# Last tokens' values stored and fetched by one transfer each, from GpSimd's queue, and the next rows' load one round earlier, in a recurrent attention kernel

## Chip, cores and metric

One core of a Trainium2 chip runs the kernel. The metric is device time in microseconds (us), the median over runs; lower is better. TensorE (PE in profiles) multiplies matrices, with its weight loads shown apart as PEld; VectorE is DVE, ScalarE is ACT, GpSimd is POOL, and SyncE (SP) only issues transfers. Each engine works through its own queue in order, and a queue that issues transfers (SyncE's, ScalarE's, GpSimd's) waits in order too.

## The reference

Four layers over 2048 tokens of 640 features, A B A B, each added to its input. Layer A is attention with a memory that is carried from segment to segment, and it holds the change:

```python
for s in range(n_seg):                        # 64 segments of 32 tokens, one after the other
    h = concatenate([mem, xs])                # 8 memory rows + 32 tokens
    q, k, v = h @ Wq, h @ Wk, h @ Wv          # 32 heads of 192
    scores = where(mask, q @ k.T * scale, -1e9)
    o = softmax(scores) @ v @ Wo
    mem, out[s] = o[:8], o[8:]                # the next segment needs mem
```

with mask true where the query is a memory row or the key is not later than the query. Here x is layer-normalised first. Layer B is a linear attention with softmax feature maps over all tokens; the change does not touch it.

## The kernel before

Layer A has two stages. The stage ahead (`A_pre`) computes K and Q of the last eight tokens of every segment, for all segments at once, and keeps them in DRAM (`kqb`). The chain (`A_chain`) then goes through the 64 segments. In each, only 32 rows are projected, the 8 memory rows and 24 tokens; what belongs to the last 8 tokens comes from DRAM: K and Q as `kqb`, values as `vb`.

The 32 heads are taken in four rounds n = 0 to 3 of eight heads, in the order 0 1 2 3 or, in odd segments, 3 2 1 0. A round projects Q, K and V (`project`, L1130), evicts them (`to_rows`, L1145; `v_rows`, L1157 and L1159), turns Q and K on VectorE (L1150), multiplies scores (L1167), takes the exponential (L1251), multiplies by the values (`attend`, L1180, and the last tokens' part L1193), scales by the reciprocal of the sums (L1200 or, in the last round, L1204; L1210), turns the result (L1351, L1359) and adds it into the segment's output W (`wo_round`, L1236). After the last round W is turned into the memory columns of the next hT (L1436, L1438), and TensorE goes on with the next segment's Q.

Beside this, per segment:

- `load_rows(s + 1)` (L1077) fetches the next segment's 24 new tokens from DRAM (`xn`) on GpSimd's queue, into `xr`; it is called in round 1. `xr` shares its place with `orow`, the output rows that `store_rows` (L1095) sends away at the next segment's start. `hx_transpose` (L1080) turns `xr` into hT on VectorE, ahead of the last round's reciprocals.
- `extra_v` (L1110) fetches the last tokens' values of a later round, `load_kqb` (L1099) their K and Q, and `extra_kq` (L1106) copies these into place; all on GpSimd.
- `next_values` (L259, `ps_x`) projects values of the last tokens of four later segments at once: one round of heads per segment, so a set of four segments takes four of them. `load_tails` and `gather_tails` (L250) fetch those tokens on SyncE's queue by four transfers straight out of `xn`, and `turn_tails` turns them. At the next segment's start `keep_values` (L1277) evicts the product on ScalarE, after `keep_rows` (L1088, L1091), `tail_rows` (L1221) and `turn_tail` (L1225); `store_waiting` calls `store_values` (L266), four transfers on SyncE's queue. The last segments of a layer have no later set and do none of this. The first sets are made at the end of `A_pre` by `first_values`.
- Weights. Most of Wq, Wk, Wv stays in SBUF; seven pieces (`SLOTS`) and part of Wo are streamed in every segment on SyncE's queue (L749, L804). `PACE` names the eleven matmuls after which one streamed load each may go: `release` makes the load wait for that step. So whatever else stands in SyncE's queue stands in front of these loads. `load_wo` (L776, L780) and `lay_out_wo` (L822) bring Wo early in a layer, and `late_wo` the rest of it during the first segment.
- `fill` (L1244) issues weight loads that have no effect on the result.

The chain's engines follow the order written in the program.

Of the kernel before, what the change touches and what calls it, by code (L numbers as in the profile page):

```python
# [22 lines left out]

FILL = {0: 65, 2: 79}
SEG_FILL = 1
# [100 lines left out]
class Kernel:  # L126
# [119 lines left out]

    def gather_tails(self, queue, into, k):
        rows = self.xn_rows[128 * k + 8:128 * k + 136, :].rearrange("(s t) (q f) -> q s t f", t=32, q=4)
        for q in range(4):
            queue.dma_start(out=into[32 * q:32 * q + 32, :], in_=rows[q, :, 24:32, :])  # L250

# [3 lines left out]
    def tail_values(self, ps, turned, r, piece):  # L255
        for i in range(self.KC):
            w = piece("V", r, i)
            for g in range(4):
                self.nc.tensor.matmul(ps[32 * g:32 * g + 32, 0:384], lhsT=turned[:, i, :], rhs=w[:, 384 * g:384 * g + 384],  # L259
                                      start=(i == 0), stop=(i == self.KC - 1), tile_position=(0, 32 * g),  # L260
                                      skip_group_check=True)

    def store_values(self, vt, k, r):
        for p in range(4):
            at = 384 * (p % 2)
            self.nc.sync.dma_start(out=self.vb_d[k, r, :, p // 2, :, at:at + 384], in_=vt[32 * p:32 * p + 32, :])  # L266

# [435 lines left out]
    def layer_A(self, xn_dram, at_dram, li, x_raw=None):  # L703
# [5 lines left out]
        self.kqb_d = dram.tile([NR, P, NSEG, 192], BF16, name=f"kqb{li}")  # L709
        self.vb_d = dram.tile([NSEG // 4, NR, 4, 2, 8, 768], BF16, name=f"vb{li}")  # L710
        self.otb_d = dram.tile([P, NSEG, 384], BF16, name=f"otb{li}")
# [54 lines left out]
        def load_wo(r, part):  # L766
            for k in part:
# [10 lines left out]
                G, j = 2 * k // 6, 2 * k % 6  # L778
                for h in range(4):
                    nc.sync.dma_start(out=into[32 * h:32 * h + 32, :].rearrange("f (j m) -> f j m", m=640),  # L780
                                      in_=wov[8 * r + 4 * G + h][:, j:j + 2, :])

# [36 lines left out]
        def lay_out_wo(r):  # L819
            for h in range(4):  # L820
                for G in range(2):
                    nc.sync.dma_start(out=self.wo_rows[r // 3, 32 * h:32 * h + 32, 3840 * G:3840 * G + 3840]  # L822
                                      .rearrange("f (j m) -> f j m", m=640), in_=wov[8 * r + 4 * G + h])

        def early_wo():
            for r in (0, 2, 1):
                load_wo(r, [k for k in range(6) if (r, k) in early])

# [12 lines left out]
    def A_pre(self, xn_dram, li, load_matrix, piece, wo_mid, wo_end, lay_out_wo, early_wo, x_raw):  # L841
# [12 lines left out]
        with ExitStack() as es:  # L854
# [112 lines left out]
            for h, ri, r in steps:  # L967
# [20 lines left out]
                if x_raw is not None and (h, ri) == (NH - 1, 0):  # L988
                    tasks += all_rows()
                if (h, ri) == (NH - 1, 1):  # L990
                    for k in range(2):
                        self.gather_tails(nc.gpsimd, self.tails_place(k), k)
                if x_raw is not None and h == NH - 1 and ri == NR - 1:
                    early_wo()
                for mi, m in enumerate("KQ"):
                    load_matrix(m, r)
                    w = [piece(m, r, b) for b in range(KC)]
                    for c0 in range(0, 12, CB):
                        ps = ps_.tile([P, 512], F32, name="ps_pre", tag="bank")
                        for i in range(CB):  # L1000
                            c = c0 + i
                            for b in range(KC):
# [7 lines left out]
                              in_=ps[:, :].rearrange("p (i t s) -> p i s t", i=CB, t=8))  # L1010
                if x_raw is not None or (h, r) == (0, 3) or r in (1, 2):
# [3 lines left out]
                if x_raw is None and h == NH - 1 and ri == NR - 1:  # L1015
                    early_wo()
                stq = nc.scalar if x_raw is None else nc.sync
                stq.dma_start(out=self.kqb_d[r, :, SH * h:SH * h + SH, :], in_=st)
                if x_raw is not None:
                    if h == 0 and ri + 1 < NR:  # L1020
                        for m in "KQV":
                            load_matrix(m, NR - 2 - ri)
                    if h == NH - 1 and ri in (1, 2):
                        lay_out_wo(3 * (ri - 1))
                    if (h, ri) == (0, 0):
                        for h1 in range(1, NH):
                            for k1 in range(NT):
                                transpose_rows(normed[h1, k1], h1, k1)
                if h == NH - 1 and ri == 1:
                    first_values(0, (3, 2))  # L1030
                    if x_raw is None:
                        load_matrix("V", 0)
                if h == NH - 1 and ri == NR - 1:
                    first_values(0, (1, 0))
                    first_values(1, (0,))
            assert not tasks
# [3 lines left out]
    def A_chain(self, xn_dram, at_dram, li, load_slot, piece, late_wo, load_both, wo, low):  # L1040
# [3 lines left out]
        with tc.tile_pool(name=f"A{li}_ch", reuse_waits="tile", bufs=1) as sp, \  # L1044
# [63 lines left out]
            def extra_v(s, n):  # L1108
                r = rounds(s)[n]
                nc.gpsimd.dma_start(out=Vs[n % 2][64:80, :].rearrange("p (q f) -> p q f", f=VH)[:, :, 0:192],  # L1110
                                    in_=self.vb_d[s // 4, r, s % 4].rearrange("g t (q f) -> (g t) q f", f=192))

# [144 lines left out]
            def load_tails(s):  # L1257
                k = set_of(s)[0]
                if (s % 4 == 3 or s == 0) and k < NSEG // 4:
                    self.gather_tails(nc.sync, xt, k)  # L1260

# [13 lines left out]
            def keep_values():  # L1275
                if waiting:
                    nc.scalar.activation(out=ots[0], in_=waiting[0][0][:, 0:384], func=ACT.Copy)  # L1277
# [14 lines left out]
            def fetch_kq(s, n):  # L1292

                at = NR * s + n + 4
                if at < len(turns):
# [7 lines left out]
            kqs.append(load_kqb(0, rounds(0)[3]))  # L1303
            load_rows(1)
            for s in range(NSEG):
                W = pop.tile([P, 512], F32, name="ps_w", tag="w")
# [16 lines left out]

                if s > 0:
                    keep_rows(W_done)
                    rows = tail_rows(rct, "OTh")
                    otb = turn_tail(rows, ots[1][:, 0:192])
                    store_rows(s - 1)
                    store_tail(otb, s - 1, rounds(s - 1)[L])
                    keep_values()  # L1330
                load_tails(s)
                turn_rows(q_or_k("Q", 0))
                store_waiting()
                if s == 0:
                    fill(FILL[li])
                turn_rows(q_or_k("K", 0))
# [31 lines left out]
                for n in range(L):  # L1368
# [165 lines left out]
```

## Time and profile before

| | |
|---|---|
| median of 3 runs | 3486.01 us (3479.56 to 3490.64) |
| profiled execution | 3475.69 us, span 3474.0 us |
| busy: PE, PEld | 3047.1 us (88%), 1953.1 us (56%) |
| busy: DVE, ACT, POOL | 2183.5 us (63%), 1909.7 us (55%), 1356.9 us (39%) |
| moved by DMA | 744.27 MB, mean 214 GB/s |
| granted TensorE clock | 0.982 of full |

The span is what the profiler saw between the first and the last instruction; the execution's own time is a little longer. Busy shares are means over the two attention layers (about 140 to 1480 and 1880 to 3225 us) and the rest. TensorE's busy time is modelled, so 88% does not mean that it works at its peak for that time. In a line of a profile "x", a count, stands after a group, and a bracket with an arrow names what ended the idle time before an instruction.

### The profile page before, as it was taken

The numbers are of one execution on the slowest core, as the hardware profiler recorded it, in microseconds if no ns is written. First come the engines' busy times: TensorE is split into PE (matmuls) and PEld (weight loads), VectorE is DVE, ScalarE is ACT, GpSimd is POOL, SyncE is SP. The second block draws the span as 40 slices with busy tenths as digits, with TensorE's granted clock in tenths as the row PEclk, the third lists the DMA queues.
The fourth block names the chain that finished last, engine by engine and source line by source line (L and its number), as shares of the span: only waits on it lengthen the run. The fifth ranks groups of instructions, "written<-read, shape, count | busy, mean of one in ns | idle before, by whom it ended". The sixth has DMA issues, their size and how long they took to land.

```text
span 3474.0 us, 145242 instructions
## 1 busy us (share of the span) xinstructions
PE 3047.1 (88%) x60832; PEld 1953.1 (56%) x61138; DVE 2183.5 (63%) x5427; ACT 1909.7 (55%) x4540; POOL 1356.9 (39%) x2808
## 2 busy tenths in 40 slices
PE   8778888888888888899987888888888888888899
PEld 6545555555555555555366555555555555555553
DVE  5456666666666666646643566666666666666565
ACT  3256555665565655556432565566555655565463
POOL 2234444444444444431110344444444444444300
PEclk9899999999999999999999999999999999999999
DMA  8867776777667776760285677677776777677600
GB/s 322 309 208 234 236 229 223 233 238 229 219 224 232 240 227 218 232 239 6 76 301 206 217 237 237 224 227 243 226 226 223 232 236 232 220 227 236 212 1 31
DMA packets 342767, 744.27 MB, mean 214 GB/s; under 512 B 71450, under 2 KB 123314, under 8 KB 339042
## 3 DMA queue, kind: packets, MB, share of 16 engines
q1 hardware_dynamic: 278210, 647.65, 55.6%
q0 software_dynamic: 61984, 74.09, 7.6%
q8 instruction: 480, 7.86, 0.9%
q10 hardware_dynamic: 1920, 13.24, 0.9%
q14 instruction: 173, 1.42, 0.1%
HBM read 665.34 MB, written 72.96 MB: 213 GB/s over the span
## 4 chain that ended last, share of the span: by engine, by line
PE 52%; DMA 30%; DVE 8%; POOL 4%; issue 3%; ACT 2%; SPq 1%; PEld 0%; POOLq 0%; DVEq 0%; ACTq 0%
DMA under<-xn 20%; PE ps_qk_q L1130 10%; PE ps_qk_k L1130 9%; PE ps_v L1130 7%; PE ps_w L1236 6%; DMA arena<-in_A_Wv_dram 4%; PE ps_s L1167 3%; PE ps_pre L1003 2%; PE kv L1489 2%; DMA arena<-wo_rows 2%; DVE raws L1436 2%; POOL kqb L1099 2%; POOL Vp L1110 2%; PE ps_wo L468 2%; DVE hT L1438 1%
## 5 line engine op out<-in xcount | busy, mean ns | idle before, releaser
L1130 PEld LDWEIGHTS <-hT 128*32 128x32 bf16 x30720 | 810.1, 97 | 578.8 <-issue 196.1
L1150 DVE STREAM_TRANSPOSE QK<-raws 128x512 bf16<-128x512 bf16 (+1 forms) x1152 | 730.1, 642 | 235.3 <-ACT raws L1145 182.6
L1130 PE MATMUL ps_qk_k<-arena,hT 128*32 128x384 bf16 x10240 | 530.2, 331 | 27.4 <-DMA arena<-in_A_Wk_dram 20.5
L1130 PE MATMUL ps_qk_q<-arena,hT 128*32 128x384 bf16 x10240 | 515.0, 330 | 44.6 <-DVE hT L1438 39.6
L1130 PE MATMUL ps_v<-arena,hT 128*32 128x384 bf16 x8192 | 454.2, 328 | 94.0 <-DMA arena<-in_A_Wv_dram 79.3
L1110 POOL DMA_DIRECT2D Vp<-vb x512 | 267.2, 522 | 653.0 <-PE ps_t L1193 383.0
L1210 ACT ACTIVATE raws<-ps_o,rc 128x192 bf16<-128x192 f32 x1024 | 373.4, 420 | 230.6 <-DVE rc L1204 224.0
L1145 ACT ACTIVATE raws<-ps_qk_k 128x512 bf16<-128x512 f32 (+1 forms) x640 | 313.5, 510 | 293.3 <-PE ps_qk_k L1130 293.3
L1106 POOL COPY QK<-kqb 64x192 bf16<-64x192 bf16 x1024 | 351.1, 343 | 284.6 <-PE ps_s L1167 241.3
L1145 ACT ACTIVATE raws<-ps_qk_q 128x512 bf16<-128x512 f32 x512 | 305.7, 597 | 130.0 <-PE ps_qk_q L1130 102.2
L1159 DVE CAST Vp<-ps_v 64x384 bf16<-64x384 f32 x512 | 286.2, 559 | 129.0 <-ACT Vp L1157 116.5
L1157 ACT ACTIVATE Vp<-ps_v 64x384 bf16<-64x384 f32 x512 | 246.4, 481 | 157.4 <-PE ps_v L1130 156.9
L1099 POOL DMA_DIRECT2D kqb<-kqb x512 | 285.4, 557 | 107.1 <-DMA kqb<-arena 43.6
L1236 PE MATMUL ps_w<-arena,under 128*32 128x320 bf16 x6144 | 309.6, 303 | 13.6 <-issue 8.1
L1095 POOL DMA_DIRECT2D attn<-under x128 | 91.7, 716 | 523.9 <-DVE under L1225 522.9
L1167 PEld LDWEIGHTS <-QK 128*80 128x80 bf16 x4096 | 196.6, 121 | 168.4 <-issue 144.2
L1167 PE MATMUL ps_s<-QK 128*80 128x80 bf16 x4096 | 257.7, 211 | 22.3 <-POOL QK L1106 21.8
L1251 ACT ACTIVATE E<-ps_s 80x320 bf16<-80x320 f32 x512 | 217.6, 425 | 51.3 <-PE ps_t L1193 28.4
L1236 PE MATMUL ps_w<-arena,QK 128*32 128x320 bf16 x3072 | 135.6, 305 | 122.9 <-DVE QK L1359 118.6
L1088 ACT ACTIVATE wh<-ps_w 64x160 f32<-64x160 f32 x256 | 76.6, 299 | 262.2 <-DVE raws L1436 260.7
L1003 PEld LDWEIGHTS <-arena 128*128 128x128 bf16 x1920 | 188.9, 99 | 44.6 <-DMA arena<-in_A_Wk_dram 12.1
L1180 PE MATMUL ps_o<-Vp,E 80*32 80x193 bf16 x4096 | 181.2, 249 | 10.7 <-issue 6.6
(159 smaller groups left out, 4341.4 us busy)
## 6 DMA issues: line engine op xcount, KB each, us to landing
arena<-wo_rows SPq DMA_DIRECT2D x536, 320.0 KB
arena<-in_A_Wq_dram SPq DMA_DIRECT2D x427, 384.0 KB
arena<-in_A_Wk_dram SPq DMA_DIRECT2D x298, 384.0 KB
arena<-in_A_Wv_dram SPq DMA_DIRECT2D x288, 384.0 KB
kqb<-kqb POOLq DMA_DIRECT2D x512, 48.0 KB, 5.6
kqb<-arena SPq DMA_DIRECT2D x8, 1536.0 KB
Vp<-vb POOLq DMA_DIRECT2D x512, 24.0 KB, 3.9
otb<-under POOLq DMA_DIRECT2D x256, 48.0 KB, 4.2
```

The costliest lines, as they stand in the source:

```text
L1003: nc.tensor.matmul(ps[:, T * i:T * i + T], lhsT=w[b][:, P * c:P * c + P], rhs=xBT[:, b, :], start=(b == 0), stop=(b == KC - 1))
L1099: nc.gpsimd.dma_start(out=kqb[:], in_=self.kqb_d[r, :, s, :])
L1106: nc.gpsimd.tensor_copy(out=o, in_=kqb[h, :].rearrange("p (x c q) -> p x c q", c=3, q=16))
L1110: nc.gpsimd.dma_start(out=Vs[n % 2][64:80, :].rearrange("p (q f) -> p q f", f=VH)[:, :, 0:192], in_=self.vb_d[s // 4, r, s % 4].rearrange( ...
L1130: last = nc.tensor.matmul(o, lhsT=hT[:, b, :], rhs=rhs, start=(i == 0), stop=(i == KC - 1), tile_position=(0, 32 * g), skip_group_check=True)
L1145: nc.scalar.activation(out=raw[:, c], in_=ps[:, c], func=ACT.Copy)
L1150: nc.vector.transpose(out=o, in_=i)
L1157: nc.scalar.activation(out=o, in_=i, func=ACT.Copy)
L1159: nc.vector.tensor_copy(out=o, in_=i)
L1167: nc.tensor.matmul(S[0:80, c0:c0 + 80], lhsT=KT[:, 4 * x + c, :], rhs=QT[:, 4 * x + c, :], start=(c % 2 == 0), stop=(c % 2 == 1), skip_gro ...
L1210: nc.scalar.activation(out=out, in_=i, func=ACT.Copy, scale=rc[G])
L1236: step = nc.tensor.matmul(W[q:q + 32, 0:320], lhsT=OT[i // 6][:, i % 6 // 2, 32 * (i % 2):32 * (i % 2) + 32], rhs=rhs, start=(first and i ...
```

## The change

- `store_values` is one transfer on GpSimd's queue in place of four on SyncE's. For this, `vb` has another order in DRAM, and `tail_values` multiplies its four groups of columns in another order. `extra_v` reads the same values by a new pattern, still one transfer.
- `keep_values` evicts and stores at once, and is called first in a segment; `store_waiting` is gone.
- A new DRAM tensor `tails_d` holds the last tokens in rows of their own. `copy_tails` fills it on GpSimd's queue: sets 0 and 1 ahead of the chain, the other sets in segment 1, two transfers a round. `load_tails` is one transfer from it, on GpSimd's queue, called at the end of the segment before.
- `load_rows(s + 1)` is called in round 0, behind `fetch_kq`, in place of round 1.
- Ahead of the chain, the first values of rounds 1 and 0 are made sooner, `load_matrix` calls change order, `load_wo` and `lay_out_wo` split their transfers along another axis (two in place of four for a piece, twelve in place of eight for a round), and `early_wo` is called in two parts.
- The long `fill` of the first segment is gone.

```diff
+    def copy_tails(self, k0, k1, ts=range(8)):
+        rows = self.xn_rows[128 * k0 + 8:128 * k1 + 8, :].rearrange("(k s t) d -> t k s d", s=4, t=32)
+        for t in ts:
+            self.nc.gpsimd.dma_start(out=self.tails_d[k0:k1, t, :, :], in_=rows[24 + t])
+
+    def load_tails(self, into, k):
+        self.nc.gpsimd.dma_start(out=into, in_=self.tails_d[k].rearrange("t s (q f) -> q (t s) f", q=4))
...
     def store_values(self, vt, k, r):
-        for p in range(4):
-            at = 384 * (p % 2)
-            self.nc.sync.dma_start(out=self.vb_d[k, r, :, p // 2, :, at:at + 384], in_=vt[32 * p:32 * p + 32, :])
+        self.nc.gpsimd.dma_start(out=self.vb_d[k, r].rearrange("c x f -> x c f"), in_=vt)
...
-                for h in range(4):
-                    nc.sync.dma_start(out=into[32 * h:32 * h + 32, :].rearrange("f (j m) -> f j m", m=640),
-                                      in_=wov[8 * r + 4 * G + h][:, j:j + 2, :])
+                for i in range(2):
+                    nc.sync.dma_start(out=into[:, 640 * i:640 * i + 640], in_=wov[8 * r + 4 * G:8 * r + 4 * G + 4, :, j + i, :])
...
                 if (h, ri) == (NH - 1, 1):
+                    self.copy_tails(0, 2)
                     for k in range(2):
-                        self.gather_tails(nc.gpsimd, self.tails_place(k), k)
-                if x_raw is not None and h == NH - 1 and ri == NR - 1:
-                    early_wo()
+                        self.load_tails(self.tails_place(k), k)
+                if h == NH - 1 and ri == NR - 1:
+                    if x_raw is not None:
+                        early_wo(True)
+                    for k in range(2):
+                        first_values(k, (0,))
...
+                if h == NH - 1 and ri == 2:
+                    first_values(0, (1,))
                 if h == NH - 1 and ri == NR - 1:
-                    first_values(0, (1, 0))
-                    first_values(1, (0,))
+                    early_wo(False)
...
             def keep_values():
                 if waiting:
-                    nc.scalar.activation(out=ots[0], in_=waiting[0][0][:, 0:384], func=ACT.Copy)
-
-            def store_waiting():
-                if waiting:
-                    _, k, r = waiting.pop()
+                    ps, k, r = waiting.pop()
+                    nc.scalar.activation(out=ots[0], in_=ps[:, 0:384], func=ACT.Copy)
                     self.store_values(ots[0], k, r)
...
+                if s == 1:
+                    self.copy_tails(2, NSEG // 4, (2 * n, 2 * n + 1))
                 at = NR * s + n + 4
...
                 if s > 0:
+                    keep_values()
                     keep_rows(W_done)
...
-                    keep_values()
-                load_tails(s)
                 turn_rows(q_or_k("Q", 0))
-                store_waiting()
-                if s == 0:
-                    fill(FILL[li])
                 turn_rows(q_or_k("K", 0))
...
                     fetch_kq(s, n)
+                    if n == 0 and 0 < s < NSEG - 1:
+                        load_rows(s + 1)
...
-                    if n == 1 and s > 0 and s + 1 < NSEG:
-                        load_rows(s + 1)
...
                 wo_round(W, order[L], OTs[L], False, True, (*range(6, 12), *range(6)))
+                load_tails(s + 1)
                 next_values(s)
```

More of the change, by code (lines that the diff above doesn't have):

```diff
@@ L819, in lay_out_wo, with early_wo @@
         def lay_out_wo(r):
[L820 to L825, printed above, removed]
+            for i in range(12):
+                nc.sync.dma_start(out=self.wo_rows[r // 3, :, 640 * i:640 * i + 640],
+                                  in_=wov[8 * r + 4 * (i // 6):8 * r + 4 * (i // 6) + 4, :, i % 6, :])
+        def early_wo(first):
+            sooner = {(0, 0), (0, 1), (2, 4), (2, 5)}
             for r in (0, 2, 1):
-                load_wo(r, [k for k in range(6) if (r, k) in early])
+                load_wo(r, [k for k in range(6) if (r, k) in early and ((r, k) in sooner) == first])
         def late_wo(r, part=range(6)):
@@ L1010, in A_pre @@
                               in_=ps[:, :].rearrange("p (i t s) -> p i s t", i=CB, t=8))
[L1011 removed]
+                if x_raw is not None and h == 0 and ri + 1 < NR:
+                    for m in "KQ":
+                        load_matrix(m, NR - 2 - ri)
+                if h == 0 and (x_raw is not None or r):
                     load_matrix("V", r)
```

21 lines of the change are left out of this document (7 added, 14 removed).

## The prediction

> **What bounds the kernel now.** I read the page first, for its chain that ended last. The second line gives the shares by line.
>
> ```profile
> span 3474.0 us, 145242 instructions
> DMA under<-xn 20%; PE ps_qk_q L1130 10%; PE ps_qk_k L1130 9%; PE ps_v L1130 7%; PE ps_w L1236 6%; DMA arena<-in_A_Wv_dram 4%; PE ps_s L1167 3%; PE ps_pre L1003 2%; PE kv L1489 2%; DMA arena<-wo_rows 2%; DVE raws L1436 2%; POOL kqb L1099 2%;
> ```
>
> A fifth of the end is set by one transfer, the fetch of the next segment's rows (`load_rows`, `under<-xn`). Next the view of waits: who waited for whom, total us, times, longest.
>
> ```profile
> DVE hT L1080 <- DMA under<-xn: 136.7, 119, 3.0
> PE ps_w L1236 <- DVE QK L1359: 118.6, 110, 3.0
> PE ps_v L1130 <- DMA arena<-in_A_Wv_dram: 79.3, 101, 1.9
> PE ps_s L1167 <- POOL QK L1106: 21.8, 2, 11.6
> PE ps_qk_k L1130 <- DMA arena<-in_A_Wk_dram: 20.5, 50, 1.1
> PE ps_w L1236 <- DMA arena<-in_A_Wo_dram: 16.6, 12, 2.3
> PE ps_pre L259 <- DVE under L253: 7.8, 3, 3.5
> ```
>
> VectorE waits for that fetch 119 times in 126 fetches (63 in each of two layers), and TensorE, in order too, then waits 110 times for the last round's turned outputs. Third comes one ordinary segment, from its chain of waits (start, us, what).
>
> ```profile
> 1191.52 6.13 DMA under<-xn
> 1197.67 0.37 DVE hT L1080
> 1198.07 0.24 DVE rc L1204 x2
> 1198.33 0.43 ACT raws L1210
> 1198.78 0.39 DVE QK L1359
> ```
>
> The timeline has what stands beside it; brackets hold the idle time before an instruction.
>
> ```profile
> 1187.35 0.56 POOL L1099 DMA_DIRECT2D kqb<-kqb  x1 [0.18 <-issue]
> 1188.42 0.74 POOL L1106 COPY QK<-kqb 64x192 bf16<-64x192 bf16 x2 [0.51 <-PE ps_s L1167]
> 1191.67 0.50 PE L1167 MATMUL ps_s<-QK 128*80 128x80 bf16 x8
> 1195.55 0.35 PE L1130 MATMUL ps_v<-arena,hT 128*32 128x384 bf16 x4 [0.84 <-DMA arena<-in_A_Wv_dram]
> 1196.46 0.56 DVE L1159 CAST Vp<-ps_v 64x384 bf16<-64x384 f32 x1 [1.03 <-ACT Vp L1157]
> 1197.12 0.35 PE L1180 MATMUL ps_o<-Vp,E 80*32 80x193 bf16 x8
> 1199.21 0.86 PE L1236 MATMUL ps_w<-arena,QK 128*32 128x320 bf16 x19 [0.70 <-DVE QK L1359]
> ```
>
> VectorE is free at 1197.02 (1196.46 + 0.56), but the rows land at 1197.65; hT, which is not needed before the next segment, stands in its order ahead of the reciprocals, whose input was ready at 1197.47. So a fetch nobody needs yet delays the last output round. TensorE stalls twice: 0.84 for the late Wv, 0.70 for this.
>
> **The change part by part.** The sum is made against the profiled execution, 3475.7 us (span 3474.0 and 1.7 around it). The median of the runs shown is 3486.0, so 10.3 is added at the end.
>
> *Next rows behind the first attention.* The one fetch moves from round 1 to round 0, behind the kqb load: 1187.35 + 0.56 = 1187.91 in place of 1191.52, so it lands by about 1194.1 with the same 6.13, 2.9 before VectorE can take it. On GpSimd's queue it is moved past one Vp load and one kqb load, and the QK copy of round 1 stands behind it: 1188.42 becomes about 1188.6, and the scores of round 2, which read it, start at 1191.67. What is late next: the reciprocals start at about 1197.5 instead of 1198.07, and TensorE's 0.70 shrinks to about 0.13. Of 118.6 us in 110 waits, 110 x 0.13 = 14 stay: **-104**.
>
> *Values stored by one transfer on GpSimd.* SyncE's queue: in a segment with stores; at the next segment's head, 20.65 later; and in one of the layer's last segments, which have no values left to make.
>
> ```profile
> 1182.33 2.50 SPq L266 DMA_DIRECT2D vb<-under  x4
> 1184.93 0.87 SPq L749 DMA_DIRECT2D arena<-in_A_Wq_dram  x2
> ```
>
> ```profile
> 1202.98 2.52 SPq L266 DMA_DIRECT2D vb<-under  x4
> ```
>
> ```profile
> 1408.46 2.44 SPq L749 DMA_DIRECT2D arena<-in_A_Wq_dram  x3
> ```
>
> The four stores hold SyncE for 2.5 us, and the second and third Wq load, with every weight load after them, stand behind. Two windows by engine show what the DMA engines do then (last columns: granted clock, DMA share, GB/s).
>
> ```profile
> 1184.30:1185.30 1.00, 1.00 (x28) 0.58 (x24) 0.76 (x2) 0.67 (x3) 0.12 (x1) 1.00 0.48 129
> 1188.30:1189.30 1.00, 1.00 (x31) 0.76 (x32) 0.87 (x2) 0.67 (x2) 0.69 (x2) 1.00 1.03 406
> ```
>
> They are half idle while SyncE issues stores, and full when the loads arrive together. Weights issued 2 us sooner use the idle part, and Wv, late by 0.84, arrives in time. The trace tries this itself: the view of TensorE's waits from 1347 to 1407, three segments with stores, has this row, while that from 1407 to 1467, three without, has no Wv or Wk row at all.
>
> ```profile
> PE ps_v L1130 <- DMA arena<-in_A_Wv_dram: 2.0, 3, 0.9
> ```
>
> I take 95 of the 99.8 (79.3 + 20.5), leaving what belongs to the first segments: **-95**. A rule of the Trainium skill speaks against this: its page "DMA: Bandwidth & Descriptors", section "Issuing engines are not separate DMA queues", says that DMAs from any engine end on the same 16 DMA engines, so that another issuer saves only its sequencer's issue time, usually small. By it the 95 would stay unearned; here that issue time is the 2.5 us of the row.
>
> The price is on GpSimd, one more store in 118 segments, about 0.56 by the kqb row, ahead of the first QK copy, which waits for the scores anyway; and on ScalarE, where the eviction of these values (L1277) now comes first. Its count, from the view of tile `under`, and rows of the segment start from the timeline:
>
> ```profile
> L1277 ACT ACTIVATE under<-ps_x x118: 481/482/490, 194.0 to 3121.0; 128x384 bf16<-128x384 f32 x118
> ```
>
> ```profile
> 1200.76 0.93 PE L259 MATMUL ps_x<-under,tT 128*32 128x384 bf16 x16
> 1201.52 0.61 ACT L1088 ACTIVATE wh<-ps_w 64x160 f32<-64x160 f32 x2 [2.46 <-DVE raws L1436]
> 1202.16 0.42 ACT L1221 ACTIVATE otr<-ps_t,rct 128x192 bf16<-128x192 f32 x1
> 1202.48 0.48 ACT L1277 ACTIVATE under<-ps_x 128x384 bf16<-128x384 f32 x1
> 1203.05 0.60 ACT L1145 ACTIVATE raws<-ps_qk_q 128x512 bf16<-128x512 f32 x1
> 1203.68 1.47 DVE L1150 STREAM_TRANSPOSE QK<-raws 128x512 bf16<-128x512 bf16 x2 [0.46 <-ACT raws L1145]
> 1205.31 0.50 PE L1167 MATMUL ps_s<-QK 128*80 128x80 bf16 x8
> ```
>
> The values end at 1201.69. Eviction, row halves and tail rows (0.48, 0.61, 0.42) after that put the Q eviction at 1203.3, 0.26 late; the turns had 0.16 of room before the scores (1203.68 + 1.47 to 1205.31). About 0.12 comes through: 118 x 0.12 = **+14** (bounds 0 and 31).
>
> *Start of each attention layer.* The view of waits has TensorE idle 21.8 us in two waits for GpSimd. The timeline of the first:
>
> ```profile
> 148.01 9.18 SPq L266 DMA_DIRECT2D vb<-arena  x12
> 158.38 1.09 PE L1167 MATMUL ps_s<-QK 128*80 128x80 bf16 x8 [10.23 <-POOL QK L1106]
> 169.12 17.31 SPq L780 DMA_DIRECT2D arena<-in_A_Wo_dram  x24
> ```
>
> GpSimd cannot fetch Vp until twelve stores have left SyncE, behind Wo pieces. They become three on GpSimd, issued a step earlier. What is late next is a Vp landing, about 1 each: **-20**. The Wo pieces go from four transfers to two, and start sooner: of the 16.6 us of waits I take **-10** (bounds 0 and 16.6). Laying out Wo goes from 8 to 12 transfers a round; the rest of the early loads only change order in a stage where TensorE is busy with ps_pre. First values ahead of the last K and Q may remove the 7.8 us at L259 or wait as long again for V's weights: taken at 0, bounds -8 and +8. The fills hide nothing once the stall is gone: 0.
>
> *Tails through rows of their own.* Ahead of the chain, eight gathers become eight copies and two loads, with one more landing between. In segment 1 each round gets two copies on GpSimd, 2 x 0.56 = 1.1 us ahead of its kqb load and QK copy, with two layers: **+2** (0 to 8). Later loads of tails leave SyncE's queue, one on GpSimd at the segment's end, where nothing is queued behind.
>
> Sum: 104 + 95 + 20 + 10 - 14 - 2 = 213. 3475.7 - 213 = 3262.7; plus 10.3 = **3273**.
>
> **The rivals.** *A, the engines and not SyncE's time hold Wv back.* The 1.03 share speaks for it, the 0.48 and the three segments without stores against. 3273 + 95 = **3368**, which is the outcome of the rule named above.
>
> *B, the rows still land late.* The fetch shares a buffer with the rows of the segment before, so it waits for their store; the view of the store's line (L1095) has how long that takes.
>
> ```profile
> DMA to landing us min/median/max: 2.9/3.5/5.9
> ```
>
> The store waits for the turned tail, about 0.4 after the tail rows' new end at 1203.3, or 1183.1 one segment earlier. It would land at 1186.6, or at 1189.0 at worst, both with room; but weights now move at that moment. If that eats the gain: 3273 + 104 = **3377**.
>
> *C, slower: that wait blocks GpSimd.* The QK copy stands behind the fetch, and needs 0.72 + 0.74 for both. With a landing of L the copy ends at 1183.1 + L + 1.46, and the scores of round 2 start at 1191.67, so harm starts at L = 7.1 and takes the whole 213 (1.7 in each of 126 segments) at L = 8.8. At 9.2: 126 x 2.1 = 265, or **3538**. No store took over 5.9.
>
> *D, it nets out*: new waits for tokens' copies and for landings on GpSimd take all back, **3486**. Nothing in the rows points there.
>
> **How the numbers follow.** Forecast 0.69, A 0.13, B 0.10, C 0.05, D 0.02, and 0.01 for other slips that end faster. The low end takes the favourable bounds: -14 for ScalarE, -6.6 for Wo, -8 for first values, -14 for the residual, -5 for the rest, 3273 - 48 = 3225. The high end is B with some of ScalarE's bound, 3385; C and D lie outside. Within 0.3% (about 10 us, what a measurement of this kernel can tell from no change) only D falls; A and B are still faster. So faster 0.93, same 0.02, slower 0.05.
>
> **What would show it.** Right: no row of VectorE's waits for `under<-xn`; the wait for the last turned outputs near 0.13 each; three Wq loads at the head of each segment and no Wv wait; the two 10 to 11 us waits gone; a segment of some 18.9 us instead of 20.5. A is seen if the Wv row stays with the Wq loads early, B if L1080 still waits, C if the scores wait for GpSimd's copy in every segment. The forecast is wrong if TensorE's waits only move to Wv's or the scores' rows.

## The result: 1.2% faster, where 6% was forecast

| | median, us | ratio to before, in the same session |
|---|---|---|
| before | 3488.32 (4 runs) | |
| changed | 3446.77 (3439.6 to 3456.28, 4 runs) | 0.9885 [0.985, 0.992] |

So the change brings about 41 us of the forecast 213, outside the range. The profiled execution is the slowest of the four, 3456.28 us, 19 under the profiled one of before, so the profiles show somewhat less than the medians. First the page of the changed kernel, its span and its chain that ended last by line.

```profile
span 3454.6 us, 143926 instructions
...
DMA vb<-under 6%; DMA arena<-in_A_Wv_dram 6%; PE ps_qk_k L1134 3%; PE ps_v L1134 3%; PE ps_w L1240 3%; PE ps_qk_q L1134 2%; DMA Vp<-vb 2%; PE ps_s L1171 1%; PE kv L1490 1%; DMA arena<-wo_rows 1%; DMA attn<-under 1%; PE ps_wo L468 1%; PE ps_o L1184 1%; DVE QK L1359 1%; PE ps_pq L519 1%
```

The fetch of rows, 20% before, is gone. In its place stands `vb<-under`, the very store that the change made one transfer. (This chain could be followed back only to 1872 us, so its shares of the span add up to less than half and can't be set beside those of before.) The view of waits (us in total, times, longest) says who waits for it:

```profile
DVE under L1351 <- DMA vb<-under: 153.0, 112, 2.6
PE ps_w L1240 <- DVE under L1351: 126.3, 111, 2.4
PE ps_w L1240 <- DMA arena<-in_A_Wo_dram: 32.7, 24, 2.0
PE ps_pre L261 <- DMA arena<-in_A_Wv_dram: 31.1, 6, 17.5
PE ps_v L1134 <- DMA arena<-in_A_Wv_dram: 19.7, 31, 1.1
PE ps_qk_q L1134 <- DMA arena<-in_A_Wq_dram: 16.0, 3, 13.5
DVE hT L1084 <- DMA under<-xn: 2.4, 4, 1.1
PE ps_s L1171 <- POOL QK L1110: 0.2, 1, 0.2
```

The waits that the prediction wanted gone are gone or small: VectorE waits 2.4 us for `under<-xn` in the segments in place of 136.7, Wv stands at 19.7 in place of 79.3, the start of a layer at 0.2 in place of 21.8. Three others are new or have grown: the turned outputs of the first round (L1351), 126.3 us; V's weights ahead of the chain (L261), 31.1; the first Q, 16.0. One segment in the timeline:

```profile
1194.77 0.52 DVE L1437 STREAM_TRANSPOSE raws<-ps_w 128x320 f32<-128x320 f32 x1 [1.28 <-PE ps_w L1240]
1196.19 2.44 SPq L750 DMA_DIRECT2D arena<-in_A_Wq_dram  x3
1196.52 0.83 POOL L266 DMA_DIRECT2D vb<-under  x1 [2.75 <-ACT under L1282]
1204.07 0.58 DVE L1351 STREAM_TRANSPOSE under<-raws 128x384 bf16<-128x384 bf16 x1 [2.09 <-DMA vb<-under]
1204.71 0.73 PE L1240 MATMUL ps_w<-arena,under 128*32 128x320 bf16 x16 [1.81 <-DVE under L1351]
```

Three Wq loads now go out at the segment's head, as forecast. But the evicted values lie in `ots[0]`, the place where the first round's outputs are turned to 7 us later, and VectorE may not write there before the store has read it. The view of the store's line has its issue and its landing:

```profile
L266 POOL DMA_DIRECT2D vb<-under x118: 825/839/849, 241.2 to 3106.2; - x118
DMA to landing us min/median/max: 5.3/6.6/9.1
```

Where the time lies, from the starts of the first Q projection and of the turns of W in the timeline of each profile (us; a chain has 63 turns of W, so 62 segments between them; its last segment has none and falls into the column behind):

| | ahead of layer 0's chain | first segment | 62 segments | to layer 2's chain | first segment | 62 segments | rest |
|---|---|---|---|---|---|---|---|
| before | 141.6 | 51.3 | 1274.7 | 414.3 | 47.6 | 1271.7 | 272.7 |
| changed | 179.8 | 59.7 | 1230.4 | 421.1 | 49.2 | 1241.5 | 272.9 |
| old stage (below) | 149.7 | 44.9 | 1240.7 | 411.1 | 45.8 | 1244.7 | 274.4 |
| two half stores (below) | 178.2 | 59.9 | 1174.3 | 422.6 | 48.0 | 1162.5 | 273.8 |
| both | 146.4 | 40.3 | 1184.2 | 412.1 | 39.3 | 1176.6 | 275.2 |

The two chains give 74 us where 183 were forecast (the terms 104 and 95, less 14 and 2), and 55 are lost ahead of them and in their first segments. These are two questions.

### The profile page after: what moved, and what is told of

It is laid out like the page before. It is cut to its first block, busy times and chain, and to the rows that moved or that the text cites. A ratio compares the mean times of both kernels' runs of the same rounds, so it can differ in the third digit from the quotient of the medians.

```text
span 3454.6 us, 143926 instructions
## 1 busy us (share of the span) xinstructions
PE 3038.8 (88%) x60832; PEld 1953.2 (57%) x60994; DVE 2161.0 (63%) x5427; ACT 1913.4 (55%) x4540; POOL 1505.1 (44%) x2986
## 5 line engine op out<-in xcount | busy, mean ns | idle before, releaser
L1134 PEld LDWEIGHTS <-hT 128*32 128x32 bf16 x30720 | 796.8, 97 | 471.0 <-issue 74.8
L1154 DVE STREAM_TRANSPOSE QK<-raws 128x512 bf16<-128x512 bf16 (+1 forms) x1152 | 714.4, 637 | 148.9 <-ACT raws L1149 107.6
L1134 PE MATMUL ps_qk_k<-arena,hT 128*32 128x384 bf16 x10240 | 519.8, 331 | 4.8 <-DMA arena<-in_A_Wk_dram 2.8
L1134 PE MATMUL ps_v<-arena,hT 128*32 128x384 bf16 x8192 | 439.0, 327 | 25.1 <-DMA arena<-in_A_Wv_dram 19.7
L1240 PE MATMUL ps_w<-arena,under 128*32 128x320 bf16 x6144 | 311.0, 303 | 153.4 <-DVE under L1351 126.3
L1240 PEld LDWEIGHTS <-under 128*32 128x32 bf16 x6144 | 149.6, 96 | 193.8 <-DVE under L1351 140.5
L266 POOL DMA_DIRECT2D vb<-under x118 | 98.8, 837 | 296.7 <-ACT under L1282 296.7
L1282 ACT ACTIVATE under<-ps_x 128x384 bf16<-128x384 f32 x118 | 58.0, 491 | 292.8 <-PE L1248 292.8
```

The source lines that it names most:

```text
L1134: last = nc.tensor.matmul(o, lhsT=hT[:, b, :], rhs=rhs, start=(i == 0), stop=(i == KC - 1), tile_position=(0, 32 * g), skip_group_check=True)
L1154: nc.vector.transpose(out=o, in_=i)
L1240: step = nc.tensor.matmul(W[q:q + 32, 0:320], lhsT=OT[i // 6][:, i % 6 // 2, 32 * (i % 2):32 * (i % 2) + 32], rhs=rhs, start=(first and i ...
```

## The experiments

Each ratio is to runs of the kernel before in the same session. The first three take the new waits at their word.

**A buffer of their own for the values.**

```diff
+        res["V", 1, 4] = res["V", 1, 3]
...
+            vkeep = self.under[:, 4608:4992]
...
-                    nc.scalar.activation(out=ots[0], in_=ps[:, 0:384], func=ACT.Copy)
-                    self.store_values(ots[0], k, r)
+                    nc.scalar.activation(out=vkeep, in_=ps[:, 0:384], func=ACT.Copy)
+                    self.store_values(vkeep, k, r)
```

> The changed kernel with the evicted values of the last tokens in a place of their own, so that round 0's turned output no longer has to wait until their store has read them. To make room, one resident piece of Wv (round 1, piece 4) is left out and piece 3 is read in its stead, so the output differs there; the instructions stay the same but for two weight loads. Theory 1 (the buffer wait costs the chain what TensorE waits in the changed kernel's profile, 126 us in 111 waits): the wait of VectorE's L1351 for the store vanishes, and the time falls by 90 to 126 us, to 3320 to 3357. Rival (the stream of weights holds the segment anyway, so that Wv or Wk is late instead): the waits turn up at the V or K matmuls, and the time falls by less than 30 us, to 3417 or more.

3461.61 us, 0.9943 [0.992, 0.9965]: no faster than the changed kernel. The wait at L1351 is gone; TensorE now waits for weights again (view of waits):

```profile
PE ps_v L1136 <- DMA arena<-in_A_Wv_dram: 57.8, 89, 1.7
```

**One for the rows too** (`xr` no longer shares its place with `orow`).

> As the run with the values in their own place (same piece of Wv left out), and the fetched rows of the next segment also in a place of their own, so that their fetch does not wait for the store of the last segment's rows and GpSimd is not held (227 us in 118 waits in the changed kernel). Theory 1: once the values' wait is gone, the QK copy behind the held fetch comes next, so this gains another 10 to 40 us over that run. Rival: GpSimd's wait lies beside other work and changes less than 10 us.

3454.04 us, 0.9918 [0.9892, 0.9944]. Wv again:

```profile
PE ps_v L1137 <- DMA arena<-in_A_Wv_dram: 86.1, 106, 1.8
PE ps_qk_k L1137 <- DMA arena<-in_A_Wk_dram: 26.9, 43, 1.8
```

So behind the buffer stand the streamed weights: TensorE's waits for Wv and Wk grow from 22.5 us in the changed kernel (19.7 and 2.8) to 113.0, where 126.3 went.

**The first values late again** (`first_values` of rounds 1 and 0 back at the end of `A_pre`).

> The changed kernel with the first values of rounds 1 and 0 made at the end of the stage ahead of the chain again, behind the last K and Q, as before the change; nothing else. Theory 2 (TensorE, in order, waits there for V's weights, which are loaded after K's and Q's: 11.8, 8.1 and 19 us in layer 0, 8.2 in layer 2): the stage shrinks by 30 to 45 us and the time falls to 3402 to 3417. Rival (the stage is longer because Wo is laid out by other transfers, or because weights come in another order): the same wait moves to the place where the values are now made, and the time changes by less than 10 us.

3460.83 us, 0.9946 [0.9919, 0.9973]. The stage ahead gets 16 us shorter (163.4), the first segments 9 and 7 longer (68.8 and 56.2): the waits only move, and the time is if anything longer than with the first values early (0.9946 against 0.9885).

**Only the rows' fetch moved** (kernel before, `load_rows` called in round 0).

> The kernel before with one edit: the next rows are fetched in round 0 behind the kqb load in place of round 1. The prediction's first term alone: VectorE's wait for the rows and TensorE's 118.6 us for the last turned output shrink to 14, and the time falls by 104 us, to 3384; the Wv waits stay at 79 us. Rival (the rows' fetch waits for the store of the rows that share its place, and holds GpSimd): GpSimd's line for the fetch shows 100 us of waits or more, and the time falls by less than 50 us.

3434.47 us, 0.9866 [0.9827, 0.9906]: about as fast as the whole change, though the term was 104 and about 47 came. The waits at L1359 fell from 118.6 to 0.4 us, and Wv took part of it back, 79.3 before:

```profile
PE ps_v L1130 <- DMA arena<-in_A_Wv_dram: 109.2, 132, 2.6
```

**One store on SyncE, alone and with the early rows.** The first is the kernel before with `store_values` as one transfer, still on SyncE's queue and at its old place; the second has the early fetch as well.

```diff
-  for p in range(4):
-      at = 384 * (p % 2)
-      self.nc.sync.dma_start(out=self.vb_d[k, r, :, p // 2, :, at:at + 384], in_=vt[32 * p:32 * p + 32, :])
+  self.nc.sync.dma_start(out=self.vb_d[k, r].rearrange("c x f -> x c f"), in_=vt)
...
```

The order of `vb` in DRAM follows, as in the change.

> The kernel before with one store of the values in place of four, on SyncE's queue and at its old place; rows still fetched in round 1. By the prediction's own term (four stores hold SyncE for 2.5 us, and so Wv and Wk come late) Wv waits fall from 79 us to under 20 and the time by 75 to 95, to 3390 to 3410. Rival (the two stalls of a segment cover each other: what Wv gives back, the wait for the rows takes): the Wv waits go, the wait for the rows grows, time within 25 of before, 3460 to 3485.

> The kernel before with the rows fetched in round 0 and one store of the values instead of four, still on SyncE's queue and at its old place. The prediction's own reason (four stores hold SyncE for 2.5 us and so the weights come late): SyncE is held for 0.9 instead, the Wv and Wk waits go from about 19 us in 20 segments to under 6, time about 3350 to 3370. Theory W: loads issued 1.6 us sooner wait for the same engines, Wv waits stay above 12 in 20 segments, time 3425 to 3440, like the run with the rows alone (3434).

Alone 3444.42 us, 0.9892 [0.9875, 0.991]; together 3360.82 us, 0.9644 [0.9609, 0.9679]. Alone, the Wv waits fall (79.3 to 21.8), the wait for the late rows grows from 118.6, and 38 us come through:

```profile
PE ps_w L1234 <- DVE QK L1357: 129.8, 114, 2.1
PE ps_v L1128 <- DMA arena<-in_A_Wv_dram: 21.8, 44, 1.0
```

Together they bring 124, more than 47 + 38: two stalls of one segment cover each other, and either, taken away alone, lets the other grow. With the rows early, three issues fewer on SyncE are worth 77 us (0.9866 to 0.9644 of 3486). SyncE's time was a cause of late weights, as the prediction had it: Wv's row falls from 109.2 to 25.7. But in the run with both, a wait of the changed kernel stands already (L1351 is L1349 there):

```profile
PE ps_w L1234 <- DVE under L1349: 105.7, 95, 2.4
```

The kernel before, with four stores, has no such row. So one transfer at the old place keeps its buffer too long on SyncE's queue as well.

**The changed kernel with its store on SyncE or on ScalarE** (one word of `store_values`).

> The changed kernel with the one store of the values issued by SyncE instead of GpSimd; all else as changed. Theory Q (the store costs because it goes through GpSimd's queue: it lands in 6.6 us, and the transfers of that queue wait for each other): the store lands in about 4 us, the wait of VectorE for its buffer (153 us in 112 waits) shrinks to under 40, the segment falls from 19.9 to about 19.3, time about 3375. Theory W (the DMA engines are full when the streamed weights arrive, whoever issues): the buffer wait may go, but Wv waits come back for it, the segment stays within 0.15 of 19.9, time 3430 to 3455.

> The changed kernel with the one store issued by ScalarE instead of GpSimd (with SyncE it took 3380). Theory T (it is the packets of GpSimd's queue): ScalarE's transfers are not on that queue, so the wait for the buffer goes from 126 us to under 40 and the weights move as with SyncE; ScalarE pays the issue, some 0.5 to 0.9 us in a place where the Q eviction stands behind it, of which 118 x 0.3 = 35 may come through: 3380 to 3420. Rival U (any store that runs beside SyncE's loads, and not ahead of them in their queue, slows them): the wait and the half rate stay, 3440 or more.

SyncE: 3380.46 us, 0.9704 [0.9671, 0.9738]. ScalarE: 3419.23 us, 0.9824 [0.9798, 0.9851]. Both beat GpSimd, and TensorE's wait for the turn at L1351 is gone from both. ScalarE pays with its own issue (0.49 us, ahead of the Q eviction): the view of waits has a row for it that the changed kernel does not have. It also has a longer wait for the fetched values, 82.1 us where it is 43.3 with SyncE, so how the 42 us between the two runs (0.0120 of 3486) are shared out is not shown.

```profile
PE ps_o L1184 <- DMA Vp<-vb: 82.1, 94, 1.9
PE ps_s L1171 <- DVE QK L1154: 51.2, 117, 0.4
```

**The buffer of its own, with the store on SyncE.** In this pair nobody waits for the buffer, so what is left is what the store does to other transfers.

> The kernel with a buffer of its own for the values (a resident Wv piece is replaced by its neighbour to make room, as in its twin, 3462 us), the store on SyncE's queue instead of GpSimd's. In this pair nobody waits for the buffer, so what differs is only what the store does to other transfers. Theory T (the store as many small packets of GpSimd's queue halves what the streamed weights move 4 to 7 us after the turn of W): Wv waits fall from 58 us to under 35, the segment from 20.0 to about 19.2, time 3375 to 3395. Rival B (the queue matters only through the wait for the shared buffer, 1.2 us a segment): the pair is equal, 3445 to 3465.

3408.48 us, 0.98 [0.9768, 0.9831], against 0.9943: 50 us by the ratios, from the queue alone. One thing weakens the runs with an own buffer: with the store on SyncE, where nobody waited for the shared buffer either, the own buffer makes the kernel 33 us slower (0.9704 to 0.98), and no run shows why. So a part of what the buffer's wait cost may be hidden in the 3461.61. The pair itself has the own buffer on both sides. The windows by engine, from 4 to 7 us after a turn of W, first with GpSimd's store and then with SyncE's (last two columns: DMA share, GB/s):

```profile
1123.30:1126.30 3.00, 3.00 (x81) 1.96 (x77) 2.17 (x5) 2.23 (x7) 1.59 (x4) 1.00 0.68 199
```

```profile
1106.10:1109.10 3.00, 3.00 (x83) 1.96 (x79) 2.17 (x5) 2.23 (x7) 1.49 (x5) 1.00 0.88 257
```

The same engines do the same work in both, but 199 GB/s move in place of 257; in the three segments after each, shares of 0.90, 0.74 and 0.78 stand against 1.03, 0.96 and 1.00. So the DMA engines have idle time while GpSimd's store is under way, although SyncE has issued the same loads by then. The trace's records of single packets say how the store runs (medians over some 50 stores between 300 and 1300 us; "side by side" is the mean number of main packets under way while there is any):

```
store issued by      main packets     side by side (mean)   first start to last end
GpSimd (changed)     20 of 4608 B     1.6                   3.6 us
SyncE                128 of 768 B     2.0                   3.5 us
ScalarE              128 of 768 B     2.1                   2.3 us
```

Beside the main packets, GpSimd's store has some 140 packets of 24 B. On each queue about two main packets, or fewer, run side by side in the mean. The store's outer axis, after `"c x f -> x c f"`, is 2 long.

**The weights' stream cut** (both buffers as above, and the Wv loads of each segment left out).

> The kernel with buffers of their own for the values and the rows, and the two streamed Wv pieces of each segment left out after the first segment (their place keeps old data, so 0.79 MB of each segment's stream is not moved). Theory W (the weights' stream holds the segment once the buffer waits are gone): the Wv waits of 86 us go, the segment falls from 20.0 to about 19.1, time about 3345. Rival G (GpSimd's issuing or its transfers hold it, the Wv wait was only the last to be seen): another wait takes the place, the segment stays above 19.7, time above 3420.

3295.38 us, 0.9455 [0.9432, 0.9478], against 3454.04 with them: once the buffers are apart, the streamed weights hold the segment.

**The old stage ahead of the chain.** First the changed kernel with `load_wo`, `lay_out_wo`, `early_wo` and the order of `A_pre` as before (the last tokens still go through `tails_d`), with the store on GpSimd and on SyncE; then, on SyncE's, with only the splitting of the Wo transfers as before.

> The changed kernel with the stage ahead of the chain (order of the first values, of the early weight loads, and the splitting of the Wo transfers) as it was before; the chain is the changed one, the store is still one on GpSimd. Theory P (the changed stage costs 38 us ahead of layer 0's chain, 8 in its first segment and 7 ahead of layer 2): 142, 51 and 414 us in those places again, time about 3395. Rival (what the old order saves comes back as waits in the first segment, as in the run with the first values late): the first segment grows by 20 or more and the time stays at 3435 to 3450.

> The changed chain with the one store on SyncE, and the stage ahead of it as it was before: the two undone parts together. If the two costs are separate (67 us for the store's queue, 40 for the stage), 3447 - 67 - 40 = 3340. If they share a cause (in both, transfers that come in many slow packets hold up the early weights), the second undoing brings under 20 more: 3360 to 3380.

> The changed kernel with the store on SyncE and only the splitting of the Wo transfers as before (eight for a round in the layout, four for a piece); first values and the order of the weight loads stay as changed. Theory S (the twelve transfers of 160 KB move 102 to 117 GB/s against some 400 before, hold SyncE for 21 and 27 us instead of 12, and the V weights and first Wq stand behind): pre and first segment together fall from 244 us to about 205, time about 3345. Rival O (the order of the loads and the first values ahead of K and Q cost it): they stay above 230, time 3365 to 3385.

3406.44 us, 0.9773 [0.975, 0.9797]; 3337.14 us, 0.9582 [0.9558, 0.9605]; 3340.18 us, 0.9589 [0.9569, 0.961]. By the ratios the old stage is worth 39 us beside GpSimd's store and 43 beside SyncE's, where the splitting of the Wo transfers alone (layout and pieces together) is worth as much (40), and the order of first values and loads nothing. Windows in the stage, in the changed kernel and in the kernel before, while SyncE issues the layout of Wo and has more to send behind it:

```profile
95.00:99.00 4.00, 4.00 (x39) 3.59 (x38) 2.63 (x8) 1.33 (x4) 0.00 (x0) 1.00 0.27 102
```

```profile
79.00:88.00 9.00, 9.00 (x84) 8.07 (x83) 5.45 (x15) 3.03 (x6) 1.81 (x4) 1.00 1.02 403
```

A quarter of the share, a quarter of the rate. The second window has other loads too, but the packet records, of 1280 B each for the layout in both kernels, set the layout apart: from 98 to 100 us of the changed kernel it alone moves, with 4.2 packets side by side and 99 GB/s; from 88 to 90 us of the kernel before it has 15.7 side by side and 371 GB/s. The twelve transfers walk an outer axis of 4 heads, the eight of before one of 32 rows. And SyncE, in order, holds V's weights behind them (timelines of the changed kernel and of the last run):

```profile
120.64 26.78 SPq L821 DMA_DIRECT2D wo_rows<-in_A_Wo_dram  x12
147.47 2.48 SPq L757 DMA_DIRECT2D arena<-in_A_Wv_dram  x3
```

```profile
109.09 11.85 SPq L823 DMA_DIRECT2D wo_rows<-in_A_Wo_dram  x8
121.65 1.87 SPq L757 DMA_DIRECT2D arena<-in_A_Wv_dram  x3
```

**The store in two halves of 64 rows**, so that the outer axis of each is 64 long: on GpSimd with all else as changed; on SyncE and on GpSimd with the old stage.

```diff
-  self.nc.gpsimd.dma_start(out=self.vb_d[k, r].rearrange("c x f -> x c f"), in_=vt)
+  for x in range(2):
+      self.nc.gpsimd.dma_start(out=self.vb_d[k, r, :, x, :], in_=vt[64 * x:64 * x + 64, :])
```

> The changed kernel with its one store of the values split in two, one for each half of the partitions, both still on GpSimd's queue (the outer axis that the transfer walks is then 64 long, not 2). Theory K (the store's outer axis of 2 puts it on two of the 16 DMA engines, where its packets run one behind the other for 4.4 us and every weight load, which needs all engines, waits for those two): spread, it is through in about 1 us, the wait for its buffer falls from 126 us to under 40, the segment from 19.9 to about 19.4; less the second issue on GpSimd (0.8 us, hidden), time 3380 to 3405. Rival Q (it is GpSimd's queue itself, its many tiny packets): two transfers are no better than one, 3440 to 3460.

> The changed chain with two half stores on SyncE and the stage ahead of it as before (its twin with one store on SyncE took 3337). Theory K: spread over all engines the store costs the weights less, but SyncE issues one more (0.5 us): 3325 to 3345. Rival Q: nothing to gain on SyncE, the second issue costs as the four did (1.65 us saved brought 74 us, so 0.5 costs about 22): 3350 to 3365.

> The changed chain with two half stores on GpSimd and the stage ahead of it as before: what the change meant to do, with both transfers that use few DMA engines mended. Theory K: 40 us below the run with the two halves alone, 3335 to 3365, about equal to one store on SyncE (3337). Rival Q: as with the old stage alone, 3400 to 3415.

On GpSimd: 3329.78 us, 0.9567 [0.9551, 0.9583], by the ratios 111 us below the changed kernel and 48 below one store on SyncE. The halves land in 3.5 us in place of 6.6, and the weights are there (DMA issues from 300 to 1300 us with the median landing last, then waits):

```profile
vb<-under POOLq DMA_DIRECT2D x104, 48.0 KB, 3.5
```

```profile
PE ps_o L1185 <- DMA Vp<-vb: 17.4, 36, 1.4
PE ps_v L1135 <- DMA arena<-in_A_Wv_dram: 11.3, 23, 0.9
PE ps_w L1241 <- DVE under L1352: 0.7, 2, 0.5
```

In the packet records the 32 packets of a pair, now of 3072 B, run 3.8 side by side and are through in 1.2 us from first start to last end, where one store took 3.6; the packets of 24 B are gone.

On SyncE it goes the other way: 3388.4 us, 0.9726 [0.9711, 0.974], where one store took 3337. There each store stands ahead of the first Wq load, which goes out about 0.6 us later with two (view of SyncE's queue in the timeline, one store and then two):

```profile
1105.61 0.48 SPq L266 DMA_DIRECT2D vb<-under  x1
1106.19 1.96 SPq L750 DMA_DIRECT2D arena<-in_A_Wq_dram  x3
```

```profile
1114.70 1.09 SPq L267 DMA_DIRECT2D vb<-under  x2
1115.90 2.07 SPq L751 DMA_DIRECT2D arena<-in_A_Wq_dram  x3
```

By the ratios these are 50 us, over 118 segments with a store 0.43 each, which fits the later Wq load; TensorE's waits for Wv rise from 37.9 to 59.3. No run shows that issue time alone. The store itself is quicker there too: the same 128 packets of 768 B run 6.5 side by side in place of 2.0 and are through in 1.1 us in place of 3.5. So on SyncE's queue more engines for the store earned nothing that outweighs the second issue.

On GpSimd with the old stage: **3267.07 us** (3262.33 to 3275.91), 0.9381 [0.9366, 0.9397], the fastest of all. Its page and waits:

```profile
span 3274.2 us, 144463 instructions
...
PE ps_qk_q L1133 11%; PE ps_qk_k L1133 10%; PE ps_v L1133 9%; PE ps_w L1239 8%; DMA Vp<-vb 5%; DMA arena<-in_A_Wv_dram 5%; PE ps_s L1170 5%; PE ps_pre L1006 4%; DMA arena<-wo_rows 3%; PE ps_o L1183 2%; PE kv L1489 2%; DVE raws L1436 2%; PE ps_wo L469 2%; DVE hT L1438 1%; PE ps_pq L520 1%
```

```profile
PE ps_o L1183 <- DMA Vp<-vb: 18.4, 30, 1.7
PE ps_w L1239 <- DMA arena<-in_A_Wo_dram: 15.7, 10, 3.0
PE ps_v L1133 <- DMA arena<-in_A_Wv_dram: 13.4, 25, 1.1
PE ps_s L1170 <- POOL QK L1109: 8.1, 1, 8.1
```

TensorE's own work now leads the chain. What separates this kernel from the change is the form of the store and of the Wo transfers, which kept to few DMA engines, and the order of the early loads, which was worth nothing beside SyncE's store.

## Why the prediction was wrong, step by step

**The step that failed** is the price of the store: "one more store in 118 segments, about 0.56 by the kqb row, ahead of the first QK copy, which waits for the scores anyway". It counted the issuing engine's time (0.84 in the end, and hidden, as said) and not the transfer: what it does on the DMA engines, when it lands (6.6 us), and who needs its buffer (126.3 us of waits). In two halves it costs 111 us less (0.9885 to 0.9567 of 3486). The same was left out where Wo's layout "goes from 8 to 12 transfers a round": some 40 us beside one store, 65 beside the halves, order of the loads included (0.9567 to 0.9381).

With both mended, 3267 stands 6 us from the forecast of 3273, and the two chains give 186 us (90.5 and 95.1), where 183 were forecast. So the gap is what these forms cost, which the sum had at next to nothing. That the total fits so closely is in part luck, since single terms were off, as follows. In the changed kernel nearly every sign of being right that the prediction named is there; the one that failed is the length of the segment, 19.9 us instead of 18.9.

**Next rows, -104.** The mechanism was right: in every kernel with the early fetch the waits for the last round's outputs are at most 2.0 us and those for `under<-xn` in the segments at most 14.9. Alone it brought 47, and Wv's wait took part of the rest (79.3 to 109.2). Of rivals B and C the wait itself came, but not the harm: GpSimd waits in every segment for the rows' store, whose landing rose from 3.5 to 5.8 in the median (views of waits and of the store's line). That is under C's 7.1; the largest, 7.9, is over it, but the scores wait 0.2 us in all for GpSimd's copy.

```profile
POOL under L1081 <- DMA attn<-under: 227.2, 118, 4.2
```

```profile
DMA to landing us min/median/max: 3.9/5.8/7.9
```

**Weights sooner, -95.** The mechanism was right, but the term was added to the first as if the two were independent. Alone it brought 38, both 124 (one store on SyncE) of 199, with 105.7 us of waits for the store's buffer in that run. In the changed kernel the Wv row did fall to 19.7, and it earned little, since the wait at L1351 stood in the same segment. In the kernel with halves and the new stage the 62 segments take 1174.3 and 1162.5 us, or 18.85 a segment (2336.8 over 124): the "some 18.9" of the prediction.

**Start of the layers, -20.** The wait went (21.8 to 0.2), but the first segments became longer, 59.7 and 49.2 in place of 51.3 and 47.6. In the last run, with the stage as before, they are 40.3 and 39.3, together 19.3 less, though 8.1 us of the wait are back; so the size came out, not shown by the path that was named.

**Wo, -10.** Wrong in sign: 32.7 in place of 16.6 with the new split, 15.7 with the old one.

**First values ahead, 0.** Right where it was tested beside the old split: 3337 and 3340 with and without the old order.

**ScalarE, +14.** Not seen: no row of scores that wait for the Q turn. With 0.49 us more on ScalarE it is there, 51.2 us in 117 waits, so the room was larger than the 0.16 counted. **Tails, +2:** the second segment, which has the copies, takes 20.9 us in place of 21.4, 1.0 above the mean segment in place of 0.9.

**The rivals.** D comes nearest, in time (3486, 39 us off) and in kind: a wait for a landing on GpSimd took most of the gain back. But it named no place and no path, and had a chance of 0.02. A (the engines and not SyncE's time) is out by its own sign: the Wv row did not stay.

The rule that the prediction weighed, in the Trainium skill's "DMA: Bandwidth & Descriptors", section "Issuing engines are not separate DMA queues", is borne out in half. That transfers from different queues interleave on the same engines agrees with the 199 against 257 GB/s. That the issue time saved is usually small is not so here: 2.0 us of it in a segment (2.5 for four stores, 0.5 for one) were worth 77 us once the rows came early. The same page, in the section "Why a DMA increments its semaphore by 16 and not by 1", says that a transfer takes as many engines as the largest number up to 16 that divides the slowest axis on both sides. By that rule the store (2 against 128) keeps to 2 engines and the layout of Wo (4) to 4; the packets side by side (at most 2.1, and 4.2) and the share of 0.27 agree, and so do the 15.7 of the layout before (32). The prediction did not apply it, and it could be read off the diff.

**Open:** with SyncE and ScalarE the store has two packets side by side as well, and with SyncE the weights beside it move faster than with GpSimd's (257 against 199 GB/s). On GpSimd's queue the halves changed both the number of engines and the packets (32 of 3072 B for a pair in place of 20 of 4608 B and some 140 of 24 B), so which of these GpSimd's queue suffers from is not told apart; on SyncE's, where the packets stayed as they were, more engines brought no gain.

## What to carry to other kernels

A transfer moved to another queue is costed three times: the issue on its engine, the landing with whoever needs its buffer, and the number of DMA engines that it can use, which the outer axis of its pattern sets; merging four transfers into one may leave it two engines. Where two stalls stand in one segment, the terms of a sum aren't independent: each alone may bring half and both together more than the two halves. A wait that is gone from the profile bears out a mechanism, and only the length of the segment shows the gain.

## What the runs showed of the hardware

Two transfers of 48 KB on GpSimd's queue were through sooner (3.5 us each to landing) than one of 96 KB (6.6 us), and their two issues took 0.56 us each against 0.84. Transfers with an outer axis of 4 had 4.2 packets of 1280 B side by side and moved 99 GB/s, where an outer axis of 32 had 15.7 such packets and moved 371. On SyncE's queue the 128 packets of the store were through in 1.1 us with outer axes of 64, and in 3.5 us with one of 2. And the same store, with nobody waiting for its buffer, cost 50 us more on GpSimd's queue than on SyncE's, or 0.42 us for each of 118 stores.
